# A prologue pipelined over two chunks: transposes in idle FFN banks, four sink-row transfers, weights and chunk 2 issued early

## The chip, the cores and the metric

One core of one Trainium2 chip. In the profiles PE is the matrix engine and PEld its loading of weights, DVE the vector engine, ACT the scalar engine, POOL the GpSimd engine, and SP the engine whose queue issues most transfers. SBUF is the memory that holds the tensors, PSUM the one into which PE writes. The metric is the device time of one execution in microseconds (us), as the median over runs on the chip; the spans of traces are 1.5 to 2 us shorter than the times of the same executions. All runs below count as fast ones unless it is said otherwise. A ratio is the mean time of one kernel's fast runs over that of the other's of the same rounds, so it is not quite the ratio of the medians that are quoted beside it.

## The reference

Attention with four sink rows and a window of 128, then a feed-forward network (FFN) that takes the maximum of three products:

```python
B, H, S, D = 4, 8, 768, 64          # d_model 512, d_ff 768, 3072 tokens
scores = scale * (q @ k.transpose(0, 1, 3, 2))
keep = is_sink | in_window          # key < 4, or 0 <= query - key < 128
scores = np.where(keep, scores, -1e9)
a = softmax(scores)
x = (a @ v).transpose(0, 2, 1, 3).reshape(B * S, H * D)
h = np.maximum(np.maximum(x @ w1, x @ w2), x @ w3)
out = h @ w_out
```

## The kernel before

It works on 12 chunks of 256 rows. A loop turn does the attention of one chunk beside the FFN of others; the prologue brings up chunks 0, 1 and 2 with a hand-written order of steps. Kx and Qx are the transposes of a chunk's k and q (x is one of two halves of the heads) with the copies out of PSUM, S a score with its exp, A a weighted sum, Z the sink scores, T a transpose of the attention output, F and Y tiles of the FFN; the letter after it is the chunk (a, b, c, d for 0 to 3). Every engine runs its own instructions in the order in which the program names them. Where two statements on different engines touch what the framework takes for the same part of a tensor, it puts a semaphore wait before the later one.

The transposed k lies in kz: even and odd heads on separate partition halves, the other half zero. The zeros of each chunk's columns are written by `zeros`, the copies by `prep`:

```python
kz = [const.tile([128, NP, 2, S], BF16, name=f"kz{i}") for i in range(2)]

def zeros(i, c, eng):
    for h in range(2):
        eng.memset(kz[i][64 - 64 * h:128 - 64 * h, :, h, c * 256:c * 256 + 256], 0.0)

def prep(ci, j, g):                       # transposes of q (j=1) or k (j=0)
    pt = ps_o.tile([128, 2, 2, 128], BF16, tag="o", name="pt")
    ...                                   # four transposes into pt
    if j == 1:
        put(nc.scalar.copy, qT[b % 2][:, 2 * g:2 * g + 2], slice(0, 128))
    else:
        for h in range(2):
            hp = slice(64 * h, 64 * h + 64)
            put(nc.vector.tensor_copy, kz[b % 2][:, 2 * g:2 * g + 2, h], hp)
```

The prologue, cut:

```python
load(1)
sink_v_init()
...
run("Sa0", a=0)
warm(3)                                   # dummy matmuls
run("Sa1 Ka1 Qa1 Sa2", a=0)
...
cast_qk(1, 0, 0, nc.gpsimd)
cast_qk(1, 1, 0, nc.gpsimd)
load_w()                                  # w1, w2, w3
...
run("Fb0 Fb3 Fb6 Fa1", a=0, b=1)
load(2, nc.vector)                        # released by a DVE memset in this place
zeros(0, 2, nc.gpsimd)                    # chunk 2's columns of kz
cast_qk(2, 0, 0, nc.gpsimd)
load_wo()
...
```

The softmax here doesn't subtract the row's maximum and nothing guards it: scores larger than these inputs give would overflow.

## Time and profile before

| | us |
|---|---|
| median of three runs (range) | 215.48 (215.05 to 216.54) |
| profiled span | 213.6 |
| first FFN matmul of the dense part (Fb0) | 31.53 |
| start of the loop | 59.50 |
| end of the loop's first turn | 75.85 |

The page gives the busy share of PE in 40 slices of 5.3 us as tenths:

```profile
PE   7566969989879999999998999999999999999992
PEclk9997999999999999999999999999999999999999
```

The first six slices, up to 32 us, are the part where PE waits, and it is there that a prologue can gain. In the fourth slice the clock fell for 3 us. From the seventh slice on PE is nearly full; the dips in the ninth, eleventh and twelfth (43 to 48 and 53 to 64 us) are the waits at the end of the prologue and the start of the loop.

### The profile page before, as it was taken

The numbers are of one execution on the slowest core, as the hardware profiler recorded it, in microseconds if no ns is written. First come the engines' busy times: TensorE is split into PE (matmuls) and PEld (weight loads), VectorE is DVE, ScalarE is ACT, GpSimd is POOL, SyncE is SP. The second block draws the span as 40 slices with busy tenths as digits, with TensorE's granted clock in tenths as the row PEclk, the third lists the DMA queues.
The fourth block names the chain that finished last, engine by engine and source line by source line (L and its number), as shares of the span: only waits on it lengthen the run. The fifth ranks groups of instructions, "written<-read, shape, count | busy, mean of one in ns | idle before, by whom it ended". The sixth has DMA issues, their size and how long they took to land.

```text
span 213.6 us, 5141 instructions
## 1 busy us (share of the span) xinstructions
PE 194.2 (91%) x2058; PEld 157.4 (74%) x2058; DVE 136.8 (64%) x293; ACT 113.3 (53%) x213; POOL 65.4 (31%) x106
## 2 busy tenths in 40 slices
PE   7566969989879999999998999999999999999992
PEld 7455858975468689789687698599698698797770
DVE  6996633795488738649658468569478288277250
ACT  2545753066564475566566476376464664754412
POOL 7456300536996334405203214115125000000000
PEclk9997999999999999999999999999999999999999
DMA  5799940997999959059079177177187200200202
GB/s 156 144 244 202 208 89 7 248 173 165 265 243 225 208 162 230 9 166 226 14 194 192 54 196 151 49 176 172 49 213 136 98 0 3 98 5 0 101 0 98
DMA packets 75335, 28.67 MB, mean 134 GB/s; under 512 B 63792, under 2 KB 72240, under 8 KB 75312
## 3 DMA queue, kind: packets, MB, share of 16 engines
q1 hardware_dynamic: 72928, 25.21, 49.4%
q0 software_dynamic: 2384, 3.15, 8.6%
q8 instruction: 16, 0.26, 0.5%
q14 instruction: 7, 0.06, 0.1%
HBM read 25.20 MB, written 6.29 MB: 147 GB/s over the span
## 4 chain that ended last, share of the span: by engine, by line
PE 55%; DVE 19%; DMA 7%; ACT 7%; POOL 6%; issue 3%; SPq 1%; DVEq 0%; POOLq 0%; ACTq 0%
PE h_ps L300 31%; PE y_ps L311 7%; DVE h_sb L306 6%; DMA v_raw<-in_v_dram 5%; DVE x_sb L277 5%; DVE e_sb L242 4%; PE st L231 3%; PE pt L196 3%; ACT e_sb L239 3%; PE o_ps L269 3%; POOL kz L103 2%; PE xt_ps L288 2%; PE st L233 2%; DMA qk_raw<-in_q_dram 2%; ACT h_sb L304 2%
## 5 line engine op out<-in xcount | busy, mean ns | idle before, releaser
L300 PE MATMUL h_ps<-xT,w 128*128 128x256 bf16 x864 | 107.4, 273 | 0.7 <-ACT xT L289 0.7
L300 PEld LDWEIGHTS <-w 128*128 128x128 bf16 x864 | 81.2, 98 | 9.5 <-issue 0.8
L239 ACT ACTIVATE e_sb<-st 128x512 bf16<-128x512 f32 (+1 forms) x96 | 53.7, 564 | 21.0 <-PE st L233 20.5
L306 DVE TENSOR_TENSOR h_sb<-h_sb,h_ps 128x512 bf16<-128x512 bf16 x72 | 49.2, 685 | 20.1 <-PE h_ps L300 16.9
L242 DVE TENSOR_TENSOR e_sb<-e_sb,msk 128x1024 bf16<-128x1024 bf16 (+1 forms) x48 | 34.0, 709 | 41.3 <-ACT e_sb L239 41.3
L174 POOL CAST qk_bf<-qk_raw 128x512 bf16<-128x512 f32 x43 | 27.9, 654 | 80.7 <-DMA qk_raw<-in_k_dram 29.2
L311 PE MATMUL y_ps<-wo,h_sb 128*128 128x512 bf16 x144 | 35.3, 379 | 0.3 <-DMA wo<-in_moe_w_out_dram 0.3
L314 ACT COPY y_sb<-y_ps 128x512 f32<-128x512 f32 x24 | 14.0, 585 | 34.7 <-PE y_ps L311 31.7
L304 ACT CAST h_sb<-h_ps 128x512 bf16<-128x512 f32 x36 | 21.1, 585 | 18.9 <-PE h_ps L300 18.7
L231 PE MATMUL st<-qT,kz 128*128 128x256 bf16 x96 | 26.5, 277 | 1.1 <-ACT qT L202 0.6
L196 PE MATMUL pt<-ident,qk_bf 128*128 128x128 bf16 x192 | 18.5, 222 | 6.2 <-POOL qk_bf L174 2.3
L311 PEld LDWEIGHTS <-h_sb 128*128 128x128 bf16 x144 | 12.6, 98 | 12.7 <-DVE h_sb L306 2.0
L277 DVE TENSOR_TENSOR x_sb<-o_ps,rc 128x256 bf16<-128x256 f32 x48 | 20.4, 424 | 1.7
L233 PE MATMUL st<-qT,kz 128*128 128x128 bf16 x96 | 21.2, 221 | 0.0
L269 PE MATMUL o_ps<-ve,e_sb 128*128 128x65 bf16 x352 | 18.4, 193 | 2.2 <-DVE e_sb L242 1.2
L180 POOL CAST ve<-v_raw 128x512 bf16<-128x512 f32 x24 | 15.4, 645 | 15.0 <-DMA v_raw<-in_v_dram 15.0
L269 PEld LDWEIGHTS <-e_sb 128*128 128x128 bf16 x352 | 16.5, 97 | 4.4 <-DVE e_sb L242 1.8
L196 PEld LDWEIGHTS <-qk_bf 128*128 128x128 bf16 x192 | 12.8, 99 | 9.0 <-POOL qk_bf L174 3.7
L204 DVE COPY kz<-pt 64x512 bf16<-64x512 bf16 x36 | 15.0, 418 | 2.4 <-PE pt L196 2.0
L229 PE MATMUL st<-qT,kz 128*128 128x128 bf16 x64 | 14.2, 222 | 0.9 <-ACT qT L202 0.8
L202 ACT COPY qT<-pt 128x512 bf16<-128x512 bf16 x6 | 4.4, 734 | 18.9 <-PE pt L196 18.9
L289 ACT COPY xT<-xt_ps 128x512 bf16<-128x512 bf16 x24 | 13.2, 596 | 1.6 <-PE xt_ps L288 1.6
(45 smaller groups left out, 142.1 us busy)
## 6 DMA issues: line engine op xcount, KB each, us to landing
v_raw<-in_v_dram SPq DMA_DIRECT2D x24, 256.0 KB
out_dram<-y_sb SPq DMA_DIRECT2D x24, 256.0 KB
qk_raw<-in_k_dram SPq DMA_DIRECT2D x36, 128.0 KB
qk_raw<-in_q_dram SPq DMA_DIRECT2D x36, 128.0 KB
w<-in_moe_w_dram POOLq DMA_DIRECT2D x3, 768.0 KB, 11.4
qk_raw<-in_k_dram SPq DMA_DIRECT2D x6, 256.0 KB
qk_raw<-in_q_dram SPq DMA_DIRECT2D x6, 256.0 KB
wo<-in_moe_w_out_dram POOLq DMA_DIRECT2D x2, 384.0 KB, 8.1
```

The lines of the kernel that those rows point to most:

```text
L174: eng.tensor_copy(bfs[ci][:, j, g].rearrange("p i (h d) -> p h i d", d=D), qk[:, j, 4 * g:4 * g + 4])
L196: nc.tensor.transpose(pt[:, i, p] if runs else pt[:, p, i], x[:, j, g, i, p * 128:(p + 1) * 128], ident)
L231: nc.tensor.matmul(st[:, 1:3], lhsT=kh[:, q0:q0 + 128], rhs=qh[:, q0:q0 + 256], start=True, stop=True)
L233: nc.tensor.matmul(st[:, 3], lhsT=kh[:, q0 + 128:q0 + 256], rhs=qh[:, q0 + 128:q0 + 256], start=True, stop=True)
L239: nc.scalar.activation(e[:, h, lo:], st[:, lo:], AF.Exp, scale=scale)
L242: nc.vector.tensor_mul(e[:, :, lo:], e[:, :, lo:], m)
L269: nc.tensor.matmul(o[:, hh], lhsT=es[ci, p][:, h, sl], rhs=ve[b % 2][:, n, 2 * p + h], start=(c == 0 and x == 0), stop=(x == len(blocks) - 1),
L277: nc.vector.tensor_mul(xs[ci, t][:, 4 * g:4 * g + 4], o[:, :, 0:D], rc.unsqueeze(2).to_broadcast([128, 4, D]))
L300: nc.tensor.matmul(hp[:, f], lhsT=w_sb[wi][:, ds, (2 * fp + f) * 128:(2 * fp + f + 1) * 128], rhs=xTs[ci][:, ds, :], start=(ds == 0), stop ...
L304: nc.scalar.copy(dst, hp)
L306: nc.vector.tensor_max(dst, dst, hp)
L311: nc.tensor.matmul(yp, lhsT=hs[ci][:, fb, t * 128:(t + 1) * 128], rhs=wo[:, fb], start=(fb == 0), stop=(fb == FB - 1))
```

## The change

Its intent: let chunk 1 arrive earlier, put its work between that of chunk 0, spread copies over DVE and ACT, and have chunk 2 in SBUF before it is wanted. The core of the diff (renamed masks, strides and dummy counts are cut):

```diff
-        raw = tc.alloc_tile_pool(name="raw", bufs=2)
+        raw = tc.alloc_tile_pool(name="raw", bufs=3)
...
-        for h in range(H):
-            nc.sync.dma_start(out=vs_raw[h * n_sink:(h + 1) * n_sink], ...)
+        for x in range(n_sink):
+            nc.sync.dma_start(out=vs_raw[x * H:(x + 1) * H], ...)
+        load(1)
...
-            pt = ps_o.tile([128, 2, 2, 128], BF16, tag="o", name="pt")
+            pt = (ps_f.tile([128, 2, 2, 128], BF16, tag="f", name="pt") if ci < 2 else
+                  ps_o.tile([128, 2, 2, 128], BF16, tag="o", name="pt"))
...
-                    put(nc.vector.tensor_copy, kz[b % 2][:, 2 * g:2 * g + 2, h], hp)
+                    put(nc.scalar.copy if ci == 0 and h else nc.vector.tensor_copy,
+                        kz[b % 2][:, 2 * g:2 * g + 2, h], hp)
...
+        for j, g in ((0, 0), (1, 0), (0, 1), (1, 1)):
+            cast_qk(1, j, g, nc.gpsimd)
+        for wi in range(3):
+            load_w(wi)
+        load(2, nc.gpsimd)
+        cast_v(1, 0, nc.gpsimd)
+        cast_v(1, 1, nc.gpsimd)
+        sink_v(0)
+        zeros(0, 2, nc.gpsimd)
+        run("Sa0 Sa1 Ka1 Sa2", a=0)
+        warm(3)
+        run("Sa3 Qa1", a=0)
...
+        run("Aa10 Qb0 Kb1", a=0, b=1)
+        run("Aa11 Sb0 Sb1", a=0, b=1)
...
-        run("Fb0 Fb3 Fb6 Fa1", a=0, b=1)
-        load(2, nc.vector)
-        zeros(0, 2, nc.gpsimd)
```

More of the change, by code (lines that the diff above doesn't have):

```diff
@@ L86, in load @@
             raws[ci] = (qk, vr)
+        R = H * n_sink
+        vs_raw = const.tile([R, B, D], F32, name="vs_raw")
         load(0)
-        vs_raw = const.tile([H * n_sink, B, D], F32, name="vs_raw")
-        for h in range(H):
-            nc.sync.dma_start(out=vs_raw[h * n_sink:(h + 1) * n_sink],
-                              in_=v[:, h, 0:n_sink].rearrange("b s d -> s b d"))
+        for x in range(n_sink):
+            nc.sync.dma_start(out=vs_raw[x * H:(x + 1) * H],
+                              in_=v[:, :, x].rearrange("b h d -> h b d"))
+        load(1)
         kz = [const.tile([128, NP, 2, S], BF16, name=f"kz{i}") for i in range(2)]
@@ L97 @@
         ve = [const.tile([128, S // 128, H, D + 1], BF16, name=f"ve{i}") for i in range(2)]
-        ks = [const.tile([128, NP * 136], BF16, name=f"ks{i}") for i in range(2)]
+        ks = [const.tile([128, NP * 130], BF16, name=f"ks{i}") for i in range(2)]
         vs = const.tile([128, B, H, D + 1], BF16, name="vs")
@@ L133, with load_w @@
         w_sb = {}
-        def load_w():
-            for wi, w in enumerate((moe_w1, moe_w2, moe_w3)):
-                wt = const.tile([128, DS, d_ff], BF16, name=f"w{wi}")
-                nc.gpsimd.dma_start(out=wt, in_=w.rearrange("(a p) f -> p a f", p=128))
-                w_sb[wi] = wt
+        def load_w(wi):
+            w = (moe_w1, moe_w2, moe_w3)[wi]
+            wt = const.tile([128, DS, d_ff], BF16, name=f"w{wi}")
+            nc.gpsimd.dma_start(out=wt, in_=w.rearrange("(a p) f -> p a f", p=128))
+            w_sb[wi] = wt
         wo = const.tile([128, FB, d_model], BF16, name="wo")
@@ L147, in load_wo @@
                     in_=moe_w_out[384 * a:384 * a + 384].rearrange("(a p) f -> p a f", p=128))
-        R = H * n_sink
         bm = const.tile([R, H], F32, name="bm")
         def sink_v_init():
-            nc.gpsimd.memset(bm, 1.0)
-            nc.gpsimd.affine_select(out=bm, in_=bm, compare_op=ALU.is_ge, fill=0.0, base=0,
-                                    pattern=[[-n_sink, H]], channel_multiplier=1)
-            nc.gpsimd.affine_select(out=bm, in_=bm, compare_op=ALU.is_ge, fill=0.0,
-                                    base=n_sink - 1, pattern=[[n_sink, H]], channel_multiplier=-1)
+            nc.gpsimd.memset(bm, 0.0)
+            for x in range(n_sink):
+                nc.gpsimd.affine_select(out=bm, in_=bm, compare_op=ALU.not_equal, fill=1.0,
+                                        base=-H * x, pattern=[[-1, H]], channel_multiplier=1)
             nc.gpsimd.memset(vs.rearrange("p b h d -> p (b h d)"), 0.0)
@@ L210, in prep @@
                     hp = slice(64 * h, 64 * h + 64)
-                    put(nc.vector.tensor_copy, kz[b % 2][:, 2 * g:2 * g + 2, h], hp)
+                    put(nc.scalar.copy if ci == 0 and h else nc.vector.tensor_copy,
+                        kz[b % 2][:, 2 * g:2 * g + 2, h], hp)
                 if c == 0:
-                    kv = ks[b % 2].rearrange("p (a y) -> p a y", y=136)
+                    kv = ks[b % 2].rearrange("p (a y) -> p a y", y=130)
                     for h in range(2):
                         nc.vector.tensor_copy(
-                            kv[:, 2 * g:2 * g + 2, 4 * h:4 * h + n_sink],
+                            kv[:, 2 * g:2 * g + 2, h:h + 8 * n_sink:8],
                             kz[b % 2][:, 2 * g:2 * g + 2, h, 0:n_sink])
@@ L241, in score @@
                 m = (msk if c > 0 else msk0).unsqueeze(1).to_broadcast([128, 2, 4 - lo, 128])
-                nc.vector.tensor_mul(e[:, :, lo:], e[:, :, lo:], m)
+                nc.vector.tensor_tensor(out=e[:, :, lo:], in0=e[:, :, lo:], in1=m, op=ALU.mult)
         def sink_score(ci):
@@ L284, in xpose @@
                 xTs[ci] = work.tile([128, DS, 256], BF16, tag="xT", bufs=3, name="xT")
-            pt = ps_o.tile([128, DS, 128], BF16, tag="o", name="xt_ps")
+            pt = (ps_f.tile([128, DS, 128], BF16, tag="f", name="xt_ps") if ci == 0 else
+                  ps_o.tile([128, DS, 128], BF16, tag="o", name="xt_ps"))
             x = xs.pop((ci, t)).rearrange("p h d -> p (h d)")
@@ L342, in run @@
                 step(f"{tok[0]}{c:02d}{tok[2:]}")
-        load(1)
         sink_v_init()
@@ L350 @@
         run("Ka0", a=0)
+        warm(4)
+        run("Qa0", a=0)
+        warm(8)
         cast_qk(0, 0, 1, nc.vector)
         cast_qk(0, 1, 1, nc.gpsimd)
-        run("Qa0", a=0)
-        warm(4)
-        run("Sa0", a=0)
-        warm(3)
-        run("Sa1 Ka1 Qa1 Sa2", a=0)
-        warm(3)
-        run("Sa3", a=0)
-        warm(6)
         cast_v(0, 0, nc.gpsimd)
         cast_v(0, 1, nc.gpsimd)
-        run("Sa4", a=0)
-        warm(6)
-        run("Sa5", a=0)
-        warm(4)
-        run("Aa00 Sa6 Aa01", a=0)
-        warm(4)
-        cast_qk(1, 0, 0, nc.gpsimd)
-        cast_qk(1, 1, 0, nc.gpsimd)
-        load_w()
-        run("Sa7 Kb0", a=0, b=1)
-        warm(6)
-        run("Aa10", a=0, b=1)
-        warm(4)
-        run("Aa11 Qb0", a=0, b=1)
-        cast_qk(1, 0, 1, nc.vector)
-        cast_qk(1, 1, 1, nc.vector)
-        sink_v(0)
+        for j, g in ((0, 0), (1, 0), (0, 1), (1, 1)):
[3 more added lines that the diff above has]
+        load(2, nc.gpsimd)
         cast_v(1, 0, nc.gpsimd)
         cast_v(1, 1, nc.gpsimd)
-        run("Sb0 Ta0 Sb1 Ta1 Kb1 Qb1 Sb2 Sb3", a=0, b=1)
-        warm(4)
-        run("Zb", b=1)
-        warm(4)
-        run("Sb4", b=1)
-        warm(6)
-        run("Ab00 Sb5 Ab01 Sb6 Fa0 Sb7 Fa3 Ab10 Fa6 Ab11 Tb0 Tb1", a=0, b=1)
-        run("Fb0 Fb3 Fb6 Fa1", a=0, b=1)
-        load(2, nc.vector)
-        zeros(0, 2, nc.gpsimd)
+        sink_v(0)
[3 more added lines that the diff above has]
+        run("Sa3 Qa1", a=0)
+        warm(4)
+        run("Sa4", a=0)
+        warm(5)
+        run("Sa5 Aa00", a=0)
+        warm(2)
+        run("Sa6 Aa01", a=0)
+        warm(2)
+        run("Sa7 Kb0", a=0, b=1)
+        warm(2)
+        run("Aa10 Qb0 Kb1", a=0, b=1)
+        warm(2)
+        run("Aa11 Sb0 Sb1", a=0, b=1)
+        warm(2)
+        run("Qb1 Sb2 Ta0 Sb3", a=0, b=1)
+        warm(3)
+        run("Ta1 Zb", a=0, b=1)
+        warm(3)
+        run("Sb4", b=1)
+        warm(3)
+        run("Ab00 Sb5 Ab01", b=1)
+        warm(3)
+        run("Sb6", b=1)
+        warm(3)
+        run("Sb7 Fa0 Ab10 Fa3 Ab11 Fa6 Tb0 Tb1", a=0, b=1)
         cast_qk(2, 0, 0, nc.gpsimd)
-        load_wo()
         cast_qk(2, 1, 0, nc.gpsimd)
@@ L396 @@
         cast_qk(2, 1, 1, nc.gpsimd)
+        load_wo()
         cast_v(2, 0, nc.gpsimd)
         cast_v(2, 1, nc.gpsimd)
-        run("Fa4 Fa7 Fb1 Fb4 Fb7 Fa2 Fa5 Fa8 Kc0 Qc0 Fb2 Kc1 Qc1 Sc0 Fb5 Sc1 Zc Sc2 Fb8", a=0, b=1, c=2)
-        load(3, nc.vector)
+        load(3, nc.gpsimd)
+        run("Fb0 Fb3 Fb6 Fa1 Fa4 Fa7 Fb1 Fb4 Fb7 Kc0 Qc0 Fa2 Kc1 Qc1 Fa5 Sc0 Sc1 Fa8 Zc Sc2 Fb2",
+            a=0, b=1, c=2)
         for c in range(CPB):
@@ L407 @@
             sink_v(b)
-        run("Sc3 Sc4 Ya0 Ac00 Sc5 Ac01 Sc6 Ya1 Sc7 Yb0 Ac10 Ac11 Tc0 Tc1 Yb1", a=0, b=1, c=2)
+        run("Sc3 Sc4 Fb5 Ac00 Sc5 Fb8 Ac01 Sc6 Ya0 Sc7 Ya1", a=0, b=1, c=2)
         load(4)
-        run("Kd0 Qd0 Kd1 Qd1", d=3)
+        run("Ac10 Ac11 Yb0 Tc0 Kd0 Tc1 Qd0 Yb1 Kd1 Qd1", b=1, c=2, d=3)
         for i in range(2, NCH):
```

## The prediction

> **What bounds the kernel now.** I read the page first: 213.6 us of span, PE busy 91%, no other engine over 64%. Then busy time by stage. The loop that makes one 256-row chunk per turn starts at about 59.5 us, so I cut there, at the turns, and inside the prologue where the dense FFN matmuls begin. Columns are stretch, length, then busy us (instructions) of PE, PEld, DVE, ACT, POOL, then PE clock, DMA share, GB/s.
>
> ```profile
> 30.50:42.00 11.50, 10.83 (x100) 9.62 (x101) 5.37 (x9) 2.41 (x5) 2.75 (x4) 1.00 0.37 104
> 42.00:59.50 17.50, 15.20 (x154) 10.60 (x152) 11.81 (x25) 10.29 (x18) 11.40 (x17) 1.00 0.96 207
> 59.50:75.85 16.35, 14.62 (x155) 11.57 (x153) 12.51 (x28) 8.39 (x17) 10.95 (x19) 1.00 1.07 219
> 107.20:122.20 15.00, 14.39 (x152) 11.59 (x150) 9.89 (x22) 8.51 (x18) 3.69 (x6) 1.00 0.59 140
> 153.90:168.60 14.70, 14.55 (x152) 11.40 (x150) 9.81 (x22) 8.39 (x17) 3.83 (x6) 1.00 0.64 150
> ```
>
> The last three are the three turns that score a first chunk of a batch (same work). The first takes 16.35 us, the others 15.00 and 14.70: 1.5 us lost just after the prologue. From 75.85 us on the loop is PE-full (15.55 of 15.65 us) and the change leaves it alone. The case is the first 76 us.
>
> Second, the chain that ended last, in order of time, in its first 64 us (start, length, what).
>
> ```profile
> 4.74 1.66 DVE qk_bf L174
> 9.88 0.73 DVE kz L202
> 10.64 0.75 DVE kz L202
> 14.91 0.64 DVE kz L202
> 15.56 0.73 DVE kz L202
> 17.53 0.74 ACT qT L202
> 30.90 0.59 ACT xT L289
> 31.53 3.67 PE h_ps L300 x32
> 38.57 11.06 DMA v_raw<-in_v_dram
> 49.68 0.63 POOL ve L180
> 50.36 0.95 POOL kz L103
> 56.98 2.09 POOL qk_bf L174 x4
> 63.98 0.53 POOL qk_bf L174
> ```
>
> Up to 31.5 us it is a latency chain through transposes, copies and softmax of chunks 0 and 1. Then the load of chunk 2, released only at 35.85 us by a DVE memset that stands behind FFN work, lands its v at 49.68; behind it in POOL's order stand 5.9 us of memsets and the casts of chunk 3, up to 63.98. This is what delays the first turn: PE waits 1.58 us for a POOL cast at 64.56.
>
> Third, the DMA side: the SP queue in time, then 1-us stretches (last two numbers are DMA share and GB/s).
>
> ```profile
> 5.87 4.15 SPq L91 DMA_DIRECT2D vs_raw<-in_v_dram  x8
> 10.06 0.39 SPq L73 DMA_DIRECT2D qk_raw<-in_k_dram  x1
> 9.00:10.00 1.00, 1.00 (x20) 0.98 (x18) 0.97 (x2) 0.55 (x1) 0.64 (x2) 1.00 0.05 11
> 10.00:11.00 1.00, 0.58 (x10) 0.40 (x8) 0.97 (x2) 0.92 (x3) 0.42 (x1) 1.00 0.02 4
> 19.00:20.00 1.00, 1.00 (x10) 0.94 (x9) 0.00 (x0) 1.00 (x3) 0.62 (x2) 0.50 1.09 195
> 30.00:31.00 1.00, 0.40 (x4) 0.28 (x5) 0.40 (x1) 0.68 (x2) 0.00 (x0) 1.00 0.02 3
> ```
>
> Eight sink-row transfers hold SP for 4.15 us (1.0 us of it waiting for chunk 0's v), so chunk 1 is issued at 10.06 and the DMA engines stand still at 9 to 11 us. They stand still again from 30 to 37 us, waiting for the late load of chunk 2.
>
> **What the Trainium skill says.** (1) "SBUF — State Buffer", Who interferes with whom: a DVE copy or cast in a two-port mode and a GpSimd instruction exclude each other; whoever starts first holds the shared ports for its whole length. The trace agrees: the DVE cast at 4.74 us took 1.65 us while POOL's memset of vs ran (4.29 to 6.11); the same cast takes 0.43 at 3.87 us. (2) "TensorE: Matmul & The Clock Gate", Part 1: after some 3.4 us of low activity the array's clock is halved until it is busy again; hence the dummy matmuls. The trace has clock 0.50 from 19 to 21 us. (3) "DMA: Bandwidth & Descriptors", Queues, rings and completion order: each DMA engine takes turns between the queues that have work. So chunk 2 on SP's queue and the weights on POOL's queue will share. The trace fits: the three weights took 8.6, 11.4 and 14.5 us to land while the rest of chunk 1 was in flight.
>
> **The change, part by part.**
>
> *Loads.* Four sink-row transfers instead of eight. In the order of instructions of the new kernel each load waits for the one eight places earlier, so chunk 1's first k waits only for chunk 0's second k, and its issue goes from 10.06 to about 5.87 + 4 x 0.3 = 7.1 us. The next three wait for chunk 0's second q (cast at 7.71) and its two v (8.83, 9.80), so they are issued at about 7.8, 8.9 and 9.9 instead of 10.5, 11.05 and 11.6. Chunk 1 is some 2 to 2.5 us earlier, in DMA time that stood still. Four POOL casts of chunk 1 (0.61 each) now precede the weights, whose issue therefore stays near 14 us (14.44 before), with less of chunk 1 beside them. Chunk 2 is let go right behind the third weight issue (2.4 us for three), at about 16.5 us instead of 35.85.
>
> *Do the weights then come too late?* The software queue held 8.6% x 213.6 = 18.4 us of 16 engines for 5 weight pieces, three quarters of it (13.8 us) for w1 to w3; a chunk's q, k, v costs about 0.494 x 213.6 x 1.57/25.2 = 6.6 us. From 14 us 13.8 + 6.6 + 1 (rest of chunk 1) at the observed share of 1.16 end at 14 + 21.4/1.16 = 32.5 us. w1, first in its queue, is due at about 22.5, and Fa0 wants it at about 23.5; w2 is wanted at about 32 and w3 at 37.5; chunk 2 at 37. All fit, w1 with little room.
>
> *Chunks 0 and 1 to the first dense FFN.* ACT takes one of two kz copies of chunk 0 (2 x 0.73 us), transposes go to the FFN's PSUM banks, and chunk 1's transposes stand earlier. Walking the new order with the old durations: kz complete at 7.0 instead of 7.8, but the first score still waits for qT (7.6). ACT then has two exps (0.44 each), the copy, two exps, qT (0.73): the fifth score comes at about 11.3, against 10.67 before, so ACT gives 0.6 us back. The last exp of chunk 0 ends at about 13.4, its mask at about 15. DVE then runs kz for Kb0 (1.46), reciprocal and multiply (0.64), kz for Kb1 (1.46), the same 0.64, two masks (0.69 each): 20.5 us, where before the second mask ended at 24.06. On ACT the eight exps of chunk 1 (0.6 each) with qT, two xT (0.6), and e_sink (0.38) end at about 24 us (27.4 before); last mask 24.7, Ab10 25.1, Fa3, Ab11, Fa6 (0.87 each) to 27.4, two transposes, ACT's copy of h and two xT (3 x 0.58): Fb0 starts at about 29.3 instead of 31.53. Gain 2.2 us.
>
> *Dense part to the loop.* PE's work from Fb0 to the loop is the same: 15 FFN tiles x 0.873 = 13.1, four output tiles x 1.30 = 5.2, chunk 2's scores 8 x 0.22 = 1.8, ten groups of transposes (four each for chunks 2 and 3, two of x) x 0.22 = 2.2, sink 0.44, weighted sums 4 x 0.35 = 1.4; total 24.1 us. It took 28.0 (31.5 to 59.5): 3.9 us of waits, behind chunk 2's late casts, its late v and the output weights (Ya0 waited for them at 49.37). Now chunk 2 is in before it is wanted, chunk 3 is released at about 37 us instead of 48.64 and POOL does its memsets by 43 us. DVE is nearly full here (twelve max at 0.69, six to eight copies, four masks, four divisions, about 19 us), so I keep 1.0 us of waits: 25.1 us, the loop starts at 54.4. Gain 2.9 us.
>
> *First turn.* Its POOL wait goes; 16.35 becomes about 14.85. Gain 1.5 us.
>
> Sum: 2.2 + 2.9 + 1.5 = 6.6 us. 215.48 - 6.6 = 208.9. A small bonus or loss: two extra selects (0.25 us each) move POOL's vs memset from 4.29 to about 4.8, past the DVE cast's start at 4.74. If the cast wins the ports it takes 0.43 and the start of the chain gains up to 0.7 us; if not it ends 0.5 us later. I put the two together at about zero to 0.2 and take 208.8.
>
> **The rivals.** *A, the weights are the new wait.* Chunk 2 shares the engines with them, and Fa0 and the eleven tiles after it need w1 and w2 in order. For: w1 has about 1 us of room, DMA share is already 1.1 to 1.3 in this stretch. Against: w1 is first and alone for about 2 us, and w2 has 2 to 3 us of room. If w1 or w2 came 2 us late the time would be about 210.8. *B, ACT or DVE binds the shortened chunk 0/1 stretch*, so that only the order changes: ACT has about 13 us of work from 8 to 24, DVE about 13 as well, both in strict order. Then Fb0 starts at 31 and only the later 4.4 us come: 210.9. *C, clock.* Fewer dummies between 14 and 22 us; a half clock over 6 us instead of 3 costs perhaps 1 us: 209.8. *D, nothing:* the loop takes the gain back, because PE-full turns start earlier but a later bound (output or loads) holds. Nothing speaks for it: DMA share is 0.57 in the loop. *E, more:* the cast wins, and the dense part runs with no waits: 206.9.
>
> **Range and chances.** The central sum has about 1.5 us of spread for the early walk and 1 us for the dense part. Two rivals at once reach about 212; 206.5 to 211.3 should hold it 8 times in 10. The 2% line is 211.17, so all but a double miss is faster: 0.86; same 0.13; slower 0.01, since every load is issued earlier or at the same time.
>
> **What would show each step.** Chunk 1's first k issued at 7 to 8 us and no DMA gap at 9 to 11; weights issued at about 14; chunk 2 at about 16.5; first Fb0 at 29.3; DVE waiting for no late chunk 2; loop start near 54.4; first turn below 15.2 us; turns from the second on unchanged (15.65). Wrong if FFN matmuls wait for a weight DMA, if PE waits behind POOL casts in the first turn, or if the clock stays at half past 24 us.

## The result and the profile after

| | before | after |
|---|---|---|
| median us (range, runs) | 216.01 (215.05 to 222.23, 4; one slow) | 222.50 (221.61 to 223.82, 4) |
| ratio of fast runs | | 1.032, 95% interval 1.024 to 1.041 |
| profiled span | 213.6 | 219.9 |

The kernel became slower by 3%. The same two rows of the page, after (slices of 5.5 us):

```profile
PE   7600578798989999999999999999999999999993
PEclk9975599999999999999999999999999999999998
```

The third and fourth slice, from 11 to 22 us, are empty, and the clock was halved in two slices. From the ninth slice on PE is nearly full. Busy time by stage of the kernel after, with the columns as in the prediction (stretch, length, PE, PEld, DVE, ACT, POOL, clock, DMA share, GB/s):

```profile
11.10:24.40 13.30, 0.03 (x1) 0.10 (x1) 1.65 (x4) 2.22 (x4) 8.93 (x14) 0.61 1.01 191
41.88:68.60 26.72, 25.07 (x248) 20.07 (x250) 16.84 (x33) 11.67 (x21) 10.45 (x18) 1.00 0.48 102
68.60:83.50 14.90, 14.29 (x151) 11.45 (x150) 11.18 (x26) 8.60 (x18) 6.99 (x11) 1.00 1.00 217
```

In the first stretch of 13.3 us PE does nothing, DVE and ACT some 2 us of work each; only POOL and the transfers go on. The other two are the dense part and the first turn. The stages of the two traces:

| stage, us | before | after | difference |
|---|---|---|---|
| start to Fb0 | 31.53 | 41.88 | +10.35 |
| Fb0 to the loop | 27.97 | 26.72 | -1.25 |
| first turn | 16.35 | 14.90 | -1.45 |
| rest | 137.75 | 136.40 | -1.35 |
| span | 213.6 | 219.9 | +6.3 |

So the later stages gained, and the first lost more than all of them gained. What the engines waited for there is in the list of waits (us in total, times, longest), kernel after, first 60 us:

```profile
ACT kz L204 <- DVE kz L204: 17.3, 2, 11.8
PE st L234 <- ACT qT L204: 14.5, 2, 13.3
...
DVE kz L204 <- POOL kz L106: 10.4, 1, 10.4
```

Read from the bottom: DVE's copy into kz waited 10.4 us for POOL's memset of kz (L106 is in `zeros`); ACT's copy into kz waited for DVE's; and ACT's copy of qT, which stands behind it, kept the next score on PE. The timeline of the four engines shows the same chain with its times (start, length; in brackets the idle time before it and what ended it). Kernel after, in one fence by engine:

```profile
10.41 0.56 DVE L245 TENSOR_TENSOR e_sb<-e_sb,msk 128x768 bf16<-128x768 bf16 x1 [1.61 <-ACT e_sb L242]
21.39 0.72 DVE L204 COPY kz<-pt 64x512 bf16<-64x512 bf16 x1 [10.42 <-POOL kz L106]
...
7.54 0.73 ACT L204 COPY kz<-pt 64x512 bf16<-64x512 bf16 x1 [5.45 <-DVE kz L204]
8.29 0.73 ACT L204 COPY qT<-pt 128x512 bf16<-128x512 bf16 x1
...
22.14 0.72 ACT L204 COPY kz<-pt 64x512 bf16<-64x512 bf16 x1 [11.83 <-DVE kz L204]
...
14.58 2.41 POOL L141 DMA_DIRECT2D w<-in_moe_w_dram  x3
...
17.01 1.18 POOL L181 CAST ve<-v_raw 128x512 bf16<-128x512 f32 x2
18.14 1.05 POOL L163 TENSOR_TENSOR vs<-vs_raw,bm 32x512 bf16<-32x512 f32 x1
...
19.40 1.95 POOL L106 MEMSET kz<- 64x1024 bf16 x2
...
24.43 0.37 PE L234 MATMUL st<-qT,kz 128*128 128x256 bf16 x1 [13.30 <-ACT qT L204]
```

POOL's memset stands behind everything that the change moved up in POOL's order: four casts of chunk 1 (the last at 14.02, as its data comes), three weight issues, two casts of v, the sink rows. It ends at 21.35 and DVE starts at 21.39. Before, DVE's copies of the same half of k ran at 9.88 to 11.37.

The two do not touch the same bytes. DVE writes, on partitions 0 to 63, columns 0 to 255 of the even heads of pairs 2 and 3; POOL zeroes, on the same partitions, columns 512 to 767 of the odd heads of all pairs. They share only the tensor. The wait was written in the program, and could be seen without a run: this is DVE's instruction 11 (memsets not counted) in the list of instructions that the built program of the new kernel gives, and below it the same place of the kernel before:

```
11 L204 TensorCopy kz0_96<-pt_249 64x2x2x128 [waits PE_49,Pool_49]
11 L202 TensorCopy kz0_92<-pt_210 64x2x2x128 [waits PE_49]
```

The list of ACT shows the second wait: its first copy into kz waits for DVE, not for PE, which had written what it copies:

```
2 L204 TensorCopy kz0_96<-pt_180 64x2x2x128 [waits DVE_49]
3 L204 TensorCopy qT0_98<-pt_194 128x2x2x128 [waits PE_49]
```

So in the timeline ACT's half copy starts at 7.54, as DVE's (6.80 to 7.51) ends; the copy of qT comes after it at 8.29, and the first score at 9.07. Before, DVE did both halves, ACT only qT, and the first score came at 7.66 (0.5 us of the difference is DVE's longer cast ahead of it, treated last among the experiments).

The transfers went as intended. SP's queue in the kernel after:

```profile
7.91 0.39 SPq L73 DMA_DIRECT2D qk_raw<-in_k_dram  x1
...
17.09 0.37 SPq L73 DMA_DIRECT2D qk_raw<-in_k_dram  x1
```

Chunk 1 is issued at 7.91 (before 10.06), chunk 2 at 17.09 (before it was released at 35.85). No FFN matmul waits for a weight.

### The profile page after: what moved, and what is told of

Its sections match the earlier page's. It is cut to its first block, busy times and chain, and to the rows that moved or that the text cites. A ratio compares the mean times of both kernels' runs of the same rounds, so it can differ in the third digit from the quotient of the medians.

```text
span 219.9 us, 5108 instructions
## 1 busy us (share of the span) xinstructions
PE 192.5 (88%) x2041; PEld 158.1 (72%) x2053; DVE 133.2 (61%) x287; ACT 114.1 (52%) x215; POOL 67.9 (31%) x112
## 4 chain that ended last, share of the span: by engine, by line
PE 60%; DVE 17%; ACT 9%; DMA 5%; POOL 3%; issue 3%; SPq 1%; DVEq 0%; ACTq 0%
PE h_ps L304 33%; PE y_ps L315 9%; DVE h_sb L310 6%; DVE e_sb L245 4%; ACT e_sb L242 4%; DVE x_sb L280 4%; PE st L234 4%; PE o_ps L272 3%; PE pt L198 3%; DMA v_raw<-in_v_dram 3%; DMA qk_raw<-in_q_dram 2%; PE xt_ps L292 2%; PE st L236 2%; ACT h_sb L308 2%; PE sk L251 1%
## 5 line engine op out<-in xcount | busy, mean ns | idle before, releaser
L245 DVE TENSOR_TENSOR e_sb<-e_sb,msk 128x1024 bf16<-128x1024 bf16 (+1 forms) x48 | 32.7, 682 | 42.5 <-ACT e_sb L242 42.4
L175 POOL CAST qk_bf<-qk_raw 128x512 bf16<-128x512 f32 x45 | 30.2, 673 | 90.1 <-DMA qk_raw<-in_k_dram 54.2
L315 PE MATMUL y_ps<-wo,h_sb 128*128 128x512 bf16 x132 | 32.7, 379 | 0.6
L272 PEld LDWEIGHTS <-e_sb 128*128 128x128 bf16 x352 | 17.0, 99 | 3.2 <-DVE e_sb L245 1.8
L234 PEld LDWEIGHTS <-kz 128*128 128x128 bf16 x96 | 9.5, 99 | 13.4 <-DVE kz L204 11.2
L206 DVE COPY kz<-pt 64x512 bf16<-64x512 bf16 x36 | 15.0, 418 | 3.1 <-PE pt L198 2.7
L204 DVE COPY kz<-pt 64x512 bf16<-64x512 bf16 x10 | 7.2, 724 | 10.5 <-POOL kz L106 10.4
## 6 DMA issues: line engine op xcount, KB each, us to landing
w<-in_moe_w_dram POOLq DMA_DIRECT2D x3, 768.0 KB, 10.9
```

The costliest lines, as they stand in the source:

```text
L175: eng.tensor_copy(bfs[ci][:, j, g].rearrange("p i (h d) -> p h i d", d=D), qk[:, j, 4 * g:4 * g + 4])
L234: nc.tensor.matmul(st[:, 1:3], lhsT=kh[:, q0:q0 + 128], rhs=qh[:, q0:q0 + 256], start=True, stop=True)
L245: nc.vector.tensor_tensor(out=e[:, :, lo:], in0=e[:, :, lo:], in1=m, op=ALU.mult)
L272: nc.tensor.matmul(o[:, hh], lhsT=es[ci, p][:, h, sl], rhs=ve[b % 2][:, n, 2 * p + h], start=(c == 0 and x == 0), stop=(x == len(blocks) - 1),
L315: nc.tensor.matmul(yp, lhsT=hs[ci][:, fb, t * 128:(t + 1) * 128], rhs=wo[:, fb], start=(fb == 0), stop=(fb == FB - 1))
```

## The experiments

The leading theory: the loss is the wait of DVE's copy for POOL's memset, made by the place of one statement in the program (10 us), with a smaller one from ACT's share of the copies (some 3 us); without both, the change does what was predicted. Rivals: the longer POOL and DMA stretch is itself too slow (then moving one statement wins little); the half clock costs the time; ACT waits because of the tensor kz; weights or another part of the change is a loss.

Three groups of runs were made, each beside its own runs of the kernel before on the same chip (the third group on another chip than the first two). Medians of before were 216.00, 215.07 and 215.80 us, with some slow runs among them. Kernels of different groups are compared by their ratios to before.

### Moving the zeroing statement alone

```diff
         sink_v(0)
-        zeros(0, 2, nc.gpsimd)
         run("Sa0 Sa1 Ka1 Sa2", a=0)
...
+        zeros(0, 2, nc.gpsimd)
         cast_qk(2, 0, 0, nc.gpsimd)
```

POOL's own order of instructions is the same in both kernels, as no POOL statement lies between the two places. The lists of the two built programs have every engine's instructions in the same order. The waits that differ are that of this DVE copy, those of the two memsets themselves, that of chunk 2's copy into kz, and two at the release of a later load.

> The new kernel with one statement moved: the zeroing of chunk 2's part of kz by POOL stands after chunk 1's transposes in program order again, as in the kernel before. POOL's own order of instructions is unchanged to the last instruction; only the wait of the DVE copy of chunk 0's second kz half for POOL goes. Theory (false wait): in the new kernel that copy started at 21.39 us, with 10.4 us of idle DVE before it; without the wait it starts at about 11.0 and all that hangs on it moves by 10.4 us, so 222.5 - 10.4 = about 212, fifth score at about 14 us, and no PE gap of 13.3 us. Rival 1 (contention: chunk 2 beside the weights and chunk 1 makes the loads late): the transfers are the same, so the time stays above 219 and another wait, for a DMA, appears before the FFN. Rival 2 (half clock): the clock follows from the PE gap, so it cannot be told from the theory by the total, but it would leave a mean clock below 0.97 here; the theory expects 0.98 to 1.0.

Measured: 211.85 us (211.09 to 212.38, 4 runs), ratio 0.984 (0.978 to 0.990). From 1.032 that is 4.8% of 216, or 10.4 us, the length of the wait. Timeline:

```profile
10.83 0.71 DVE L204 COPY kz<-pt 64x512 bf16<-64x512 bf16 x1
...
13.87 0.27 PE L234 MATMUL st<-qT,kz 128*128 128x256 bf16 x1 [2.79 <-ACT qT L204]
```

DVE's copy now starts as soon as DVE is free, at 10.83 instead of 21.39. The fifth score comes at 13.87 instead of 24.43. POOL's memset starts at 21.40, 2 us later than in the kernel after, because now it waits for DVE's copies; no engine stood still for it. The first score is still late, at 9.02, and Fb0 starts at 31.62, as before the change. The big loss is settled; the gain of 2.2 us in the early stretch is not there yet.

### Splitting kz into two tensors, the statement left where it was

```diff
-kz = [const.tile([128, NP, 2, S], BF16, name=f"kz{i}") for i in range(2)]
+kz = [[const.tile([128, NP, S], BF16, name=f"kz{i}{h}") for h in range(2)] for i in range(2)]
-        eng.memset(kz[i][64 - 64 * h:128 - 64 * h, :, h, c * 256:c * 256 + 256], 0.0)
+        eng.memset(kz[i][h][64 - 64 * h:128 - 64 * h, :, c * 256:c * 256 + 256], 0.0)
```

The copies and the scores use `kz[..][h]` in the same way. Now DVE's copy and the memset on the same partitions are in different tensors.

> The new kernel with the zeroing where it stands, early, but with kz held as two tensors, one for the even heads and one for the odd. The bytes that the early zeroing writes were never those that the copies of chunk 0 write, and with two tensors the order of instructions has no wait of the DVE copy for POOL. If the wait was false and is the cause: as the run with the late zeroing, 211 to 213 us. If the early position of the zeroing itself costs (POOL busy, shared ports): above 215. Rival of contention: above 219.

Measured: 211.63 us (211.41 to 212.71, 4), ratio 0.984 (0.979 to 0.990).

```profile
10.82 0.72 DVE L204 COPY kz<-pt 64x512 bf16<-64x512 bf16 x1
```

DVE waits for POOL no more, with the statement in its early place. So the wait was a false one: it came from sharing a tensor, not from data. The wait of ACT stayed (list of waits, first stretch):

```profile
ACT kz L204 <- DVE kz L204: 6.7, 2, 5.4
```

The two half copies no longer share the tensor that they write; all that they still share is the PSUM tile pt that they read. The rival that kz makes ACT wait is out.

### Both copies back on DVE as well ("the mended kernel")

The moved statement of the first experiment, and:

```diff
-                    put(nc.scalar.copy if ci == 0 and h else nc.vector.tensor_copy,
+                    put(nc.vector.tensor_copy,
```

> The run with the late zeroing, and both kz copies of chunk 0 on DVE again, as before the change. In the new kernel the ACT copy did not run beside the DVE copy but after it (DVE 6.80 to 7.51, ACT 7.54 to 8.27), and ACT's copy of qT came after that (8.29 to 9.02), so the first score stood at 9.07 us against 7.66 before. Theory: with the copies on DVE, qT starts when its transposes are done (about 7.4) and the first score comes at about 8.3; the second group gains as much again: 0.7 to 1.5 us faster than the late zeroing alone, so about 210.5 to 211.3. My prediction's view (ACT relieves DVE and the two run side by side): 0.5 to 1 us slower than the late zeroing alone.

Measured: 208.82 us (208.01 to 210.99, 4), ratio 0.972 (0.959 to 0.985): by the medians 3.0 us faster than the first experiment's kernel, twice the gain that was expected, but the two intervals overlap. It was run again in the third group, for a narrower interval:

> The mended kernel (late zeroing, both kz copies on DVE) a second time, beside the others of this call, because its first interval was 0.9585 to 0.9846: 208 to 209.5 us, ratio 0.967 to 0.975.

Measured: 208.45 us (207.94 to 209.06, 6), ratio 0.967 (0.965 to 0.970), now clear of the first experiment's. In the first of the two runs the fifth score starts at 11.30:

```profile
11.30 0.27 PE L234 MATMUL st<-qT,kz 128*128 128x256 bf16 x1 [0.80 <-ACT qT L204]
```

against 13.87 with the split copies, and the first score at 8.19 against 9.02; Fb0 at 28.21 (28.79 in the second) against 31.62. The copy that was to take work from DVE cost the chain some 3 us: it ran after DVE's anyway, and it stood ahead of ACT's exps and of qT.

### The same statement moved in the kernel before

If the place of a statement makes the wait, then the old kernel must catch it too. Its POOL statements up to the zeroing of chunk 2 were moved up ahead of Ka1 in the program, without change of their order on POOL:

```diff
         cast_qk(0, 1, 1, nc.gpsimd)
+        cast_v(0, 0, nc.gpsimd); cast_v(0, 1, nc.gpsimd)
+        cast_qk(1, 0, 0, nc.gpsimd); cast_qk(1, 1, 0, nc.gpsimd)
+        load_w()
+        sink_v(0)
+        cast_v(1, 0, nc.gpsimd); cast_v(1, 1, nc.gpsimd)
+        zeros(0, 2, nc.gpsimd)
         run("Qa0", a=0)
```

(and taken out below).

> The kernel before, with the suspected wait alone put in: the POOL statements up to the zeroing of chunk 2's part of kz are written ahead of chunk 0's second transposes. POOL's order of instructions stays that of the kernel before; the one new wait on the path is that of the DVE copy (at 9.88 us before) for POOL's zeroing, which comes behind chunk 1's v cast (19.69 to 20.30), so ends at about 22.3. Theory (false wait): DVE stands still for some 12 us and the time goes from 215.5 to 225 to 228. Rivals (contention of loads, early weights, transposes in other banks): none of these is in this kernel, so it stays within 1% of 215.5.

Measured: 228.42 us (225.78 to 232.19, 4; one slow), ratio 1.057 (1.044 to 1.071).

```profile
21.77 1.48 DVE L202 COPY kz<-pt 64x512 bf16<-64x512 bf16 x2 [12.21 <-POOL kz L103]
```

One new wait of 12.21 us, and the fast runs are 12.5 us longer in the mean (227.5 against 215.0). In the lists of the two programs every engine's order is the same, and this is the only instruction up to Fb0 that gained a wait. The wait alone accounts for such a loss; nothing else of the change is needed.

### The half clock

The kernel of the first experiment has half clock at about 15 to 21 us, the mended one does not. To tell whether its 3 us are clock or order, 40 dummy matmuls were added to the first experiment's kernel ahead of the fifth score:

```diff
         run("Sa3 Qa1", a=0)
-        warm(4)
+        warm(44)
         run("Sa4", a=0)
```

> The run with the late zeroing (kz copies split between DVE and ACT), with 40 more dummy matmuls (about 2.3 us) put into PE's wait of 2.8 us ahead of the fifth score. In that run the clock was at half from about 15 to 21 us. Question: how much of the 3 us between it and the mended kernel is the half clock that follows PE's wait, and how much the order of the copies itself. Theory (mostly the copies; PE is not the bound there): clock near 1.0, 210.5 to 211.5 us. Rival (mostly the clock): 208.5 to 210.

Measured: 212.35 us (210.90 to 213.04, 6), ratio 0.984 (0.980 to 0.988), the same as without the dummies, although the mean clock of the profiled run was 0.999 instead of 0.980. It lies above both ranges that were expected. Two of its runs at clock 1.0 took 212.6 us.

```profile
13.89 0.27 PE L234 MATMUL st<-qT,kz 128*128 128x256 bf16 x1 [0.58 <-ACT qT L204]
```

The fifth score comes where it came without the dummies (13.87). It does so in the kernel with the split tensor too (13.87), where the half clock runs from 10 to 16.5 us. So the 2.6 us up to this score are not clock. In the profiled run Fb0 comes at 30.51 instead of 31.62, so up to 1.1 us after the score may be clock in that one trace; the ratios don't show it.

### Each other part of the change undone, from the mended kernel

Chunk 2 released by DVE after the first FFN tiles, as before:

```diff
-        load(2, nc.gpsimd)                # behind the weight issues
...
+        run("Fb0 Fb3 Fb6 Fa1", a=0, b=1)
+        load(2, nc.vector)
         zeros(0, 2, nc.gpsimd)
         cast_qk(2, 0, 0, nc.gpsimd)
```

The four FFN tiles were taken out of the run below.

> From the mended kernel (late zeroing, both kz copies on DVE; 208.8 us): chunk 2 is let go where the kernel before lets it go, by a DVE memset behind the fourth dense FFN tile of chunk 1, at about 32 us instead of 17. My theory of the dense part (chunk 2 in early is worth about 2.9 us there plus 1.5 us in the first turn): 211 to 213.5 us. Rival (chunk 2 beside the weights costs as much as it gives, the share of DMA being full from 15 to 35 us): 208 to 209.5.

Measured: 210.93 us (209.48 to 211.47, 6), ratio 0.980 (0.976 to 0.984). Chunk 2 is issued at 32.97, and PE waits four times, 1.5 us in all, for POOL's casts of it.

The eight sink transfers and their old layout back (cut: the masks and strides that belong to the layout went back too):

```diff
-        for x in range(n_sink):
-            nc.sync.dma_start(out=vs_raw[x * H:(x + 1) * H], ...)
+        for h in range(H):
+            nc.sync.dma_start(out=vs_raw[h * n_sink:(h + 1) * n_sink], ...)
```

> From the mended kernel: the sink rows in eight transfers with the old layout again, so chunk 1's first k is issued near 10.0 us instead of 7.36, and the weights about 1.5 us later. Theory (the early walk needs chunk 1 and w1 earlier): 209.3 to 211 us. Rival (the walk through chunk 0 and 1 is bound by DVE and ACT, so chunk 1's time has slack): 208.3 to 209.2.

Measured: 211.45 us (210.41 to 212.12, 6), ratio 0.982 (0.978 to 0.986). SP is busy with the sinks for 4.15 us again, chunk 1 is issued at 10.25, the weights behind its casts at 18.02 instead of 15.15, and Fb0 comes at 30.86 instead of 28.79. It does so although the first score comes earlier, at 7.58 instead of 8.11, as the old masks take less of POOL's time.

The transposes of chunks 0 and 1 back in the banks of ps_o (cut: those of chunk 0's x too):

```diff
-            pt = (ps_f.tile([128, 2, 2, 128], BF16, tag="f", name="pt") if ci < 2 else
-                  ps_o.tile([128, 2, 2, 128], BF16, tag="o", name="pt"))
+            pt = ps_o.tile([128, 2, 2, 128], BF16, tag="o", name="pt")
```

> From the mended kernel: the transposes of chunks 0 and 1 and of chunk 0's x use the two banks of the weighted sums again. Theory (each transpose then waits until an older bank has been emptied by DVE or ACT, in strict order, as PE did in the kernel before at 16.34 and 17.08 us): 209.8 to 212 us. Rival (the banks do not matter since DVE is the bound of that stretch): within 0.5 us of 208.8.

Measured: 210.94 us (210.28 to 211.83, 6), ratio 0.981 (0.978 to 0.984). Fb0 comes at 30.48.

Each of the three parts is worth 0.8 to 1.1% against the mended kernel's ratio in the first group (0.972), or 1.3 to 1.5% against that of the third (0.967). The mended kernel was not in their group, so the size stays that rough; none of the three is a loss. The new order of the steps and the move of chunk 1's last casts from DVE to POOL were not undone alone.

Weights ahead of chunk 1's last two casts, to try the rival that they come too late:

```diff
-        for j, g in ((0, 0), (1, 0), (0, 1), (1, 1)):
-            cast_qk(1, j, g, nc.gpsimd)
+        cast_qk(1, 0, 0, nc.gpsimd)
+        cast_qk(1, 1, 0, nc.gpsimd)
         for wi in range(3):
             load_w(wi)
+        cast_qk(1, 0, 1, nc.gpsimd)
+        cast_qk(1, 1, 1, nc.gpsimd)
```

> From the mended kernel: the weights are issued after the first two of chunk 1's four casts, as in the kernel before, so about 2 us earlier, in competition with the rest of chunk 1. Theory (w1 has slack: landed at about 21.6, wanted at 22.5): the casts of chunk 1's second half come up to 2.4 us later, chunk 1's transposes with them, 209 to 211 us. Rival (the weights bind): 207 to 208.5.

Measured: 209.26 us (208.21 to 212.21, 6; one slow), ratio 0.971 (0.967 to 0.974). The weights are issued at 12.40 instead of 15.15 and nothing is gained; the ratio lies 0.3% above the mended kernel's of the same group, with intervals that overlap. Weights were not what bounds.

### DVE's second cast beside POOL's memset of vs

In the new kernel and all those made from it so far, but for the one with eight sink transfers (1.67 us), DVE's cast of q takes about 2.15 us beside the 1.82 us memset of vs on POOL (4.69 to 6.84 in the mended kernel). First the memset was put later, ahead of the sink rows:

```diff
 def sink_v_init():
-    nc.gpsimd.memset(vs.rearrange("p b h d -> p (b h d)"), 0.0)
...
         cast_v(1, 1, nc.gpsimd)
+        nc.gpsimd.memset(vs.rearrange("p b h d -> p (b h d)"), 0.0)
         sink_v(0)
```

> From the mended kernel: POOL's memset of vs (1.82 us, at 4.82) stands after the issue of the weights instead of at the start. In the mended kernel the DVE cast at 4.76 us takes 2.17 us, ending with that memset, while the same cast at 3.90 takes 0.43. Theory (the two exclude each other): the cast takes 0.43 to 0.6, the first score comes at about 6.8 instead of 8.19 us, and the time falls by 0.7 to 1.5 us to about 207.5. Rival (later links of the chain, chunk 0's second q at 6.84 or chunk 1, hold everything): the first score is early but the FFN starts at 28.2 as before, time 208.5 to 209.

Measured: 209.63 us (209.04 to 213.84, 6; two slow), ratio 0.974 (0.970 to 0.977). The profiled run is one of the slow ones, so only its shape is read:

```profile
4.74 0.43 DVE L174 CAST qk_bf<-qk_raw 128x512 bf16<-128x512 f32 x1 [0.43 <-DMA qk_raw<-in_q_dram]
...
22.88 0.37 PE L263 MATMUL o_ps<-vs,e_sink 128*128 128x260 bf16 x1 [3.81 <-POOL vs L166]
```

The cast took 0.43 us, as hoped. But the memset now stood in front of the sink rows on POOL, and PE waited 3.8 us for them. A wait was removed and another took its place, and the time of the fast runs did not fall (whether the new wait is as long in those is not shown). So the memset was put earlier instead, right behind the identity, ahead of the masks:

```diff
+        nc.gpsimd.memset(vs.rearrange("p b h d -> p (b h d)"), 0.0)
         msk = const.tile([128, 4, 128], BF16, name="msk")
...
-            nc.gpsimd.memset(vs.rearrange("p b h d -> p (b h d)"), 0.0)
```

> From the mended kernel: POOL's memset of vs is the first thing after the identity, ahead of the masks, so it is over before the DVE cast at 4.7 us and not late for the first weighted sum of chunk 1, which is what cost 3.8 us of PE in the run with the late memset. Theory (the cast and the memset exclude each other, and the early chain is the bound): cast 0.43 to 0.9 us, first score at about 6.8 instead of 8.19, FFN of chunk 1 at about 27 instead of 28.2, time 207 to 208. Rival (chunk 1's loads bind next): FFN at 28.2 and 208.5 to 209.

Measured: 207.73 us (207.54 to 208.74, 6), ratio 0.965 (0.962 to 0.967).

```profile
4.63 0.75 DVE L175 CAST qk_bf<-qk_raw 128x512 bf16<-128x512 f32 x1 [0.35 <-DMA qk_raw<-in_q_dram]
...
27.66 8.02 PE L304 MATMUL h_ps<-xT,w 128*128 128x256 bf16 x72 [1.21 <-ACT xT L293]
```

The cast is 1.4 us shorter, the first score comes at 6.70 instead of 8.11, and Fb0 at 27.66 instead of 28.79. This version beats both kernels. Against the mended kernel of the same group it is about 0.7 us faster by the medians; the intervals of the two ratios overlap, and Fb0 differs by 0.6 us between the two traces of the mended kernel alone (28.21 and 28.79). So the earlier first score is shown, and the size of the gain is not.

## Why the prediction was wrong, and where it was right

*Loads.* Right. Chunk 1 was issued at 7.91 (predicted 7.1), the standstill of the DMA engines at 9 to 11 us is gone (DMA share 0.67 and 1.09 in those two microseconds), the weights were issued at 14.58 (about 14), chunk 2 at 17.09 (16.5).

*Weights in time.* Right. They took 7.0, 10.9 and 15.9 us to land after issue, no FFN matmul waited for them, and issuing them 2.75 us earlier won nothing. Rival A is out.

*Chunks 0 and 1 to the first dense FFN.* This is the step that failed. It "walked the new order with the old durations": each engine's order, and the data that each instruction needs. It took for granted that DVE's copy of "kz for Ka1" would start when DVE is free. The list of instructions said otherwise: that copy had gained a wait for POOL, and POOL's memset now stood behind casts, weight issues and sink rows that kept POOL until 19.4 us. Fb0 came at 41.88 and not at 29.3. Of the 12.6 us between, 10.3 went with the false wait (41.88 to 31.62 when the statement was moved), and 2.8 to 3.4 with the second error in the same step: "kz complete at 7.0 instead of 7.8" assumed that ACT's half copy would run beside DVE's. It started when DVE's ended, complete at 8.27, and pushed qT back by as much. With both taken out the walk was good, even a little too cautious: the fifth score at 11.30 (predicted 11.3), Fb0 at 28.2 to 28.8 (29.3). But the mended kernel has both copies on DVE, which is not what was walked: halves that run side by side were in no run.

*Dense part.* Right in direction, too large. Windows of the mended kernel, second run:

```profile
28.79:55.60 26.81, 25.25 (x251) 20.15 (x251) 17.18 (x33) 11.75 (x21) 19.22 (x30) 1.00 0.97 199
55.60:70.30 14.70, 14.55 (x153) 11.51 (x151) 10.62 (x26) 8.59 (x19) 6.59 (x11) 1.00 0.95 214
```

26.8 us, not 25.1. The mis-sized term is the "total 24.1" of PE work: it measured 25.25, and 1.6 us of waits instead of 1.0. The window of the kernel before had the work at 25.66 us and could have been read instead of summed by hand. It would have shown that only 2.3 us of its 28.0 were waits, not the 3.9 of the text, so that a gain of 2.9 could not come from waits alone.

*First turn.* Right: 14.90 (mended 14.70) against 14.85 predicted, and PE's wait of 1.6 us for POOL's casts is in neither.

*Cast and memset of vs.* The memset did start later, but the cast did not win: 2.19 us in place of 1.66, ending at 6.87 instead of 6.40. That is the "0.5 us later" of the text.

*The sum.* In the mended kernel the stages give, against before, 2.7 (start to Fb0), 1.2, 1.65 and 0.7 (rest), together 6.3 us for the predicted 6.6; its time was 208.45 for the predicted 208.8. So the working comes close to a kernel that lacks the two waits, and the change as written has them. That the sum is so near is partly luck: the dense part gave 1.7 us less than predicted, and the early part 0.5 and the rest of the loop 0.7 more. The rest was to stay as it was; why it gained was not traced.

*Rivals and chances.* B named ACT and DVE for the early stretch, but as engines with too much work; both had idle time, and the trouble was what they waited for. C, the clock, was there (half clock in two slices), but it fell at 14 us, 3 us after PE had run dry. None of the rivals was a new wait. The 0.01 for slower rested on "every load is issued earlier or at the same time", which speaks of loads alone; it said nothing of the waits between engines, which a reordering can make anew.

What stays open is whether the hardware would let ACT and DVE empty one PSUM tile side by side. In every run here the program itself had the wait in it. And the parts' own worths are known to about half a per cent only.

## What to carry to other kernels

When statements are moved in a program whose waits are placed for you, compare the waits of every instruction on the critical chain in the new list of instructions with those of the old one. A statement's place makes waits even for engines whose own order it does not change, and a shared tensor is enough for one: here a memset of other bytes cost 10 us, and moving its line, or holding even and odd heads in two tensors, took it away. Before a copy is split over two engines, check that the halves may run at the same time, and what stands behind them on the engine that is to help.

## What the Trainium skill lacked or had wrong

- No page says that a wait can come from two writes of disjoint bytes in one tensor in SBUF, or that the program order alone sets its direction. Runs: 10.4 us (the change), 12.2 us (the same in the kernel before), none with the tensor split. In the new kernel the two memsets of the zeroing wait for different engines (one for ACT, one for DVE), so partition halves are told apart, and interleaved columns are not; how exactly columns are compared was not tried. "Perfetto Trace Analysis", Identifying Dependency Chains, does say to look at the semaphores in an instruction's text; the same look before the first run would have shown this wait.
- "PSUM — Partial Sum Buffer", PSUM bank collisions raise a hardware error, has it that two engines may use one bank at the same time in different quadrants of partitions. The copies here read partitions 0 to 63 and 64 to 127 of one PSUM tile and ran one after the other in every kernel that split them (6.80 to 7.51 and 7.54 to 8.27), by a wait in the program. So no run here tests the page's sentence. The page does not warn that such a split may win nothing; it cost about 3 us.
- "SBUF — State Buffer", Who interferes with whom: that DVE's cast and POOL's memset exclude each other agrees with all traces: the cast takes 0.43 us alone and 1.65 to 2.19 beside the 1.82 us memset, and then ends 0.28 to 0.29 us after it. But that whoever issues first gets the ports, as the page has it, cannot be checked on the records: in the kernel after the cast's record starts at 4.68 and the memset's at 4.77, and the cast still ended after the memset (6.87 and 6.59).
